# The sign of float64 weights carried through a rounding step, and newly written instruction lists, in a GateLoop and maxout kernel

## The chip, the cores and the metric

The kernel runs on one core of one Trainium2 chip. The metric is the device time of one execution in microseconds (us), lower is better. The profiled execution is a single one, recorded on that core.

## The reference, cut to what matters

First a GateLoop attention block: for each of 4 batches and 8 heads, over 768 positions with head size 48, a complex gate `a` (real part `a_re`, imaginary part `a_im`) is normalised, and a 48 x 48 state is turned and shrunk by it and added to.

```python
mag = np.sqrt(a_re * a_re + a_im * a_im)
scale = np.minimum(mag, 0.999) / (mag + 1e-06)
a_re_n, a_im_n = (a_re * scale, a_im * scale)
...
S_re, S_im = (new_re + kv, new_im)
y[:, :, t] = np.einsum('bhd,bhde->bhe', q[:, :, t], S_re)
```

Then its output, laid out as 3072 tokens of 384 features, goes through a feed-forward block that takes the larger of three products (384 to 768) and multiplies it by a fourth matrix (768 to 384).

```python
h = np.maximum(np.maximum(x @ w1, x @ w2), x @ w3)
return (h @ w_out).astype(np.float32)
```

The four weight matrices arrive as float64 (a float32 draw times a float64 scalar), so the kernel has to turn them into float32 by itself. [...]

## The kernel before, in words

**Tiling.** A group `g` (0 to 11) is 64 positions of all heads; a group has two halves `c` (x and y), of two batches each. For a group the kernel computes the gates (logarithms, exponentials, an arctangent) on 128 x 768 tiles, then turns q and k by running sums of the angles, forms masked scores in blocks (A, B), the outputs y, the state update dk, and then the feed-forward block: up projections `U`, maxima `u`, and the down projection by seven half-size products (Strassen's scheme: sums `S`, products `P`, result additions `r`). Group 0 goes through plain projections instead (`U..x`, `U..y`, `Ox`, `Oy`), with its two halves apart, since it starts while weights are still being prepared. The maximum is rewritten: w2 and w3 are replaced by their differences to w1, and w1 is multiplied into the output matrix in advance (entries `T`, `t`, `M`, `m`).

**Order of the work.** Nothing is scheduled by the hardware or by a loop. The string `SCHEDULE` (L21) lists about 1,750 entries of the form `name:group`. `run` (L972) takes them in order, and each emits one or more instructions. `Bound` (L187 to L205) ties each instruction to the one before it on the same engine, so the list is the order of every engine's queue: PE, DVE, ACT, POOL, and SP for most loads. An engine waits at the head of its own queue until the operands are there. All instructions pass through one helper line, so the profile puts them all at L198, and they are told apart by tile names. `SLOTS` (L116) names the PSUM slot of each successive product. `OTHER` (L122) is the set of entries that use their second choice of engine: copies out of PSUM, absolute values and the maximum with zero go to DVE in place of ACT; loads of q, k and v are issued by POOL in place of SP; additions of one tile to another are done by DVE in place of an accumulating DMA issued by POOL.

**Weights.** The weights come in twelve blocks of 128 x 768 values (`WL0` to `WL11`), each loaded as pairs of 32-bit words (768 KB) into a room that is free at the time (`ROOMS`, L129; the room called S is the tile `strassen`, H is `xhx`). `weight_step` (L419) then makes float32 of each pair with bit operations, in five steps. A high word, read as a float32, has the sign, 8 of the 11 exponent bits, and the upper mantissa.

- `Wa` (ACT): absolute value of the high word, times 2^-112, which takes the exponent offset off; it reads every second word of the room and writes a dense scratch tile `ex`.
- `Wb` (DVE): minimum with a constant, dense, in place.
- `Wc` (DVE): shift left by 3 (for blocks 0, 3 and 6, which are wanted negative, the sign bit is set as well).
- `We` (DVE): the low word shifted right by 29 is or-ed in; it reads every second word.
- `Wf` (DVE): the sign bit of the high word is xor-ed in, and the result is written to its place.
- `Wg` (six of the blocks): the block of w1 is added, by POOL's DMA or by DVE.

**Other entries that the prediction speaks of.** `Lnop` and `addw` are additions in the gates that go by accumulating DMA or DVE; `Q1`, `Q2`, `QB`, `KB`, `QG` scale copies of Q and K on DVE; `Kc` and `Qc` copy the transposed K and Q out of PSUM; `Ox:0` is the second plain output projection of group 0; the final entries `ox`, `oy`, `oz` add the last products into the output tile and `Dx`, `Dy`, `Dz` store it.

Of the kernel before, what the change touches and what calls it, by code (L numbers as in the profile page):

```python
# [21 lines left out]
Lix:0 sqi0:0 Zf:0 Zg:0 Lrx:0 xor0:0 sqr0:0 Liy:0 Lry:0 sqi1:0 add0:0 lnL0:0 expe0:0 expw0:0 xor1:0 lne0:0 relu0:0  # L22
Lnop0:0 WL0:0 sqr1:0 Wa0:0 add1:0 CL:0 lnL1:0 expe1:0 Lkx:0 abs0:0 Lix:1 Wb0:0 Wc0:0 We0:0 WL3:0 half0:0 expw1:0 Fx:0
lne1:0 relu1:0 Lnop1:0 pw0:0 Wa3:0 Wf0:0 abs1:0 Wb3:0 half1:0 WL6:0 lnw0:0 expL0:0 f3x:0 Liy:1 f2x:0 Lrx:1 Wc3:0 Wa6:0
f1x:0 Lry:1 mulai0:0 mulw0:0 We3:0 Wb6:0 WL9:0 pw1:0 lnw1:0 stt0:0 expL1:0 mulw1:0 f0x:0 atan0:0 mulai1:0 Wf3:0 T0:0
sqi:1 stt1:0 turn0:0 Wc6:0 atan1:0 Lqy:0 sumsx:0 csx:0 turn1:0 We6:0 Lqx:0 sqr:1 add:1 Wf6:0 Wa9:0 Wb9:0 WL11:0 WL10:0
xor:1 Enx:0 Eqx:0 lnL:1 Wc9:0 Ekx:0 tx:0 relu:1 mkx:0 csy:0 expe:1 We9:0 nfx:0 expw:1 sumsy:0 Lix:2 ty:0 Wf9:0 abs:1
T2:0 nfy:0 mqx:0 half:1 afx:0 Wa10:0 Wa11:0 Lvy:0 t2:0 Wb10:0 Wb11:0 Wc10:0 Wc11:0 We10:0 sax:0 We11:0 pw:1 sbx:0
uqx:0 tpqx:0 lnw:1 t0:0 Wf11:0 WL1:0 T1:0 WL2:0 Wf10:0 expL:1 Qcx:0 Lky:0 ukx:0 tpkx:0 mulw:1 Wa1:0 t1:0 Cdx:0 Lvx:0
Eqy:0 Kcx:0 Wa2:0 lne:1 Q2x:0 Fy:0 f2y:0 Wb1:0 f1y:0 WL4:0 kEnx:0 Q1x:0 M0:0 f3y:0 Liy:2 f0y:0 Eny:0 mulai:1 Wb2:0  # L30
afy:0 Ax:0 Wc1:0 stt:1 We1:0 mqy:0 Wc2:0 Wf1:0 We2:0 Eky:0 say:0 QBx:0 sqi:2 KBx:0 Lnop:1 sby:0 Wa4:0 Wf2:0 g0x:0
dkx:0 Lrx:2 Lry:2 sqr:2 add:2 atan:1 lnL:2 Wb4:0 Cdy:0 turn:1 WL5:0 Wg1:0 Wc4:0 M1:0 h1x:0 expe:2 cs:1 relu:2 g1x:0
Liy:3 expw:2 t:1 Wa5:0 abs:2 lne:2 We4:0 g2x:0 mky:0 Wf4:0 uky:0 M2:0 g3x:0 Bx:0 Wb5:0 nfx:1 Wc5:0 m1:0 Z3:0 b1x:0
tpky:0 Zh:0 uqy:0 nfy:1 b0x:0 tpqy:0 We5:0 Wg4:0 Lix:3 F:1 Kcy:0 yx:0 Lqy:1 Qcy:0 Wf5:0 xor:2 m0:0 Q2y:0 xx:0 addw:2
Q1y:0 KBy:0 WL7:0 f1:1 f0:1 QBy:0 Wg2:0 sumsx:1 Enx:1 WL8:0 half:2 Cdx:1 Ekx:1 Cdy:1 U11x:0 u11x:0 Lqx:1 lnw:2 Ay:0
Wa7:0 g0y:0 Eqx:1 expL:2 af:1 U01x:0 Wb7:0 f2:1 u01x:0 U02x:0 g1y:0 By:0 mulai:2 Wg5:0 g2y:0 Wc7:0 Wa8:0 g3y:0 We7:0
b0y:0 Lky:1 b1y:0 kEny:0 Wf7:0 sumsy:1 f3:1 yy:0 mulw:2 xy:0 sb:1 dky:0 u02x:0 stt:2 U02y:0 Lkx:1 h1y:0 Z4:0 mqx:1
atan:2 U11y:0 Lnop:2 Wb8:0 mkx:1 turn:2 sa:1 ukx:1 u11y:0 U01y:0 U12y:0 u01y:0 Eky:1 uqx:1 u02y:0 Eqy:1 cs:2 u12y:0
tpqx:1 Wc8:0 We8:0 mky:1 Eny:1 Lky:2 tpkx:1 Qcx:1 Wf8:0 t:2 Wg7:0 U21y:0 Wg8:0 U21x:0 nfy:2 nfx:2 Q1x:1 Lqx:2 mqy:1
Q2x:1 kEnx:1 uqy:1 u21y:0 U22y:0 u22y:0 u21x:0 af:2 Kcx:1 sumsx:2 F:2 Ax:1 g0x:1 g1x:1 g2x:1 Ekx:2 Enx:2 Eqx:2 Z2:0  # L40
Lvx:1 f1:2 f3:2 KBx:1 h0x:1 uky:1 tpqy:1 f2:2 Qcy:1 Q1y:1 g3x:1 Oy:0 Lvy:2 tpky:1 Q2y:1 mqx:2 Lvy:1 f0:2 Lkx:2 sa:2
sqi:3 oy:0 Lry:3 J3:0 QBx:1 dkx:1 Bx:1 sb:2 h1x:1 U12x:0 QBy:1 uqx:2 QGx:1 U22x:0 Kcy:1 KBy:1 Lrx:3 Lqy:2 u22x:0
u12x:0 Ay:1 b1x:1 g0y:1 g1y:1 g2y:1 g3y:1 b0x:1 mkx:2 sqr:3 tpqx:2 Qcx:2 By:1 yx:1 add:3 lnL:3 QBx:2 expe:3 b0y:1
sumsy:2 xx:1 Eqy:2 Eky:2 expw:3 relu:3 Q1x:2 b1y:1 QGy:1 abs:3 Ox:0 Q2x:2 Lix:4 ukx:2 ox:0 mky:2 mqy:2 Dy:0 uky:2 yy:1
addw:3 tpky:2 lne:3 kEny:1 tpkx:2 Liy:4 Lnop:3 xy:1 xor:3 half:3 Cdy:2 Kcy:2 U11:1 Cdx:2 J1:0 U01:1 Lqx:3 Lrx:4 uqy:2
lnw:3 Kcx:2 KBx:2 J2:0 expL:3 u11:1 Dx:0 Eny:2 mulw:3 mulai:3 stt:3 kEny:2 h0y:1 tpqy:2 atan:3 Lry:4 sqi:4 turn:3
Qcy:2 dky:1 h1y:1 kEnx:2 sumsx:3 u01:1 J4:0 cs:3 Eqx:3 mqx:3 Ax:2 h0y:2 Ekx:3 t:3 sqr:4 add:4 g0x:2 g1x:2 g2x:2 U12:1
Enx:3 Lrx:5 nfx:3 U02:1 lnL:4 expe:4 Q1y:2 nfy:3 expw:4 u12:1 S3:1 af:3 dky:2 g3x:2 relu:4 abs:4 addw:4 Q2y:2 F:3
u02:1 Bx:2 Ay:2 Lvx:2 sb:3 S1:1 f2:3 Lkx:3 h1y:2 f1:3 QGx:2 Lqy:3 P5:1 S2:1 P7:1 f0:3 QBy:2 g0y:2 KBy:2 g1y:2 f3:3
S4:1 lnw:4 g2y:2 P1:1 expL:4 h0x:2 P6:1 r1:1 b0x:2 b1x:2 g3y:2 r6:1 dkx:2 r5:1 r7:1 lne:4 Lry:5 sa:3 Lky:3 r57:1 h1x:2  # L50
sumsy:3 By:2 xor:4 mkx:3 b1y:2 b0y:2 Eny:3 half:4 Cdy:3 Liy:5 yx:2 xx:2 mulw:4 Eky:3 Eqy:3 Py:1 QGy:2 Px:1 P4:1 P3:1
yy:2 ukx:3 uqx:3 xy:2 oy:1 tpkx:3 tpqx:3 mky:3 h0x:3 mulai:4 Kcx:3 Lix:5 sqi:5 stt:4 Qcx:3 Lqx:4 Lky:4 P2:1 uky:3
Lnop:4 atan:4 U01:2 ox:1 u01:2 tpky:3 Lvy:3 QGx:3 Kcy:3 mqy:3 Cdx:3 uqy:3 tpqy:3 turn:4 sumsx:4 Qcy:3 Lrx:6 kEny:3
KBx:3 h0y:3 Lkx:4 Q2y:3 QBx:3 Ekx:4 Enx:4 Q1y:3 Eqx:4 cs:4 F:4 f1:4 mkx:4 t:4 sqr:5 U11:2 u11:2 Lqx:6 f3:4 Q2x:3 f2:4
Dy:1 nfx:4 Q1x:3 nfy:4 Ay:3 add:5 g0y:3 Ax:3 f0:4 g0x:3 g1y:3 g2y:3 af:4 mqx:4 xor:5 Bx:3 g3y:3 sb:4 KBy:3 U02:2 sa:4
g1x:3 U12:2 ukx:4 u02:2 S3:2 g2x:3 tpkx:4 g3x:3 Lvx:3 uqx:4 Lvy:4 lnL:5 expw:5 relu:5 Lqy:4 u12:2 expe:5 Kcx:4 tpqx:4
Qcx:4 dky:3 kEnx:3 dkx:3 S1:2 h1y:3 sumsy:4 S2:2 P5:2 h1x:3 Eqy:4 QBy:3 Dx:1 abs:5 Liy:6 addw:5 b0x:3 b1x:3 lne:5
Lnop:5 half:5 Eky:4 mky:4 Eny:4 mqy:4 Cdx:4 S4:2 Cdy:4 P1:2 P6:2 Py:2 P4:2 r1:2 yx:3 r6:2 r5:2 By:3 lnw:5 expL:5 b0y:3
mulw:5 uqy:4 h0x:4 b1y:3 mulai:5 QGy:3 Px:2 stt:5 atan:5 Lix:6 P3:2 Lry:6 xx:3 sqr:6 Liy:7 P7:2 r7:2 Lkx:5 uky:4 P2:2
tpqy:4 Lky:5 Qcy:4 r57:2 tpky:4 yy:3 sqi:6 ox:2 Lqx:5 kEnx:4 kEny:4 Lvx:4 dkx:4 oy:2 add:6 xy:3 Kcy:4 sumsy:5 turn:5  # L60
sumsx:5 h1x:4 QGx:4 Dy:2 Dx:2 Ekx:5 cs:5 Q1y:4 lnL:6 Lix:7 Eqx:5 U11:3 mkx:5 expw:6 Lvx:5 relu:6 KBx:4 Q2x:4 Enx:5
expe:6 lne:6 h0y:4 Q2y:4 mqx:5 Eky:5 U01:3 Lnop:6 abs:6 Q1x:4 u11:3 t:5 nfy:5 nfx:5 Eny:5 QBx:4 u01:3 Eqy:5 mky:5
xor:6 Ax:4 af:5 g0x:4 addw:6 sb:5 dky:4 h1y:4 sa:5 F:5 half:6 f3:5 uqx:5 g1x:4 g2x:4 lnw:6 expL:6 U12:3 u12:3 f2:5
Lrx:7 f0:5 f1:5 U02:3 tpqx:5 g3x:4 mulai:6 uky:5 tpky:5 Qcx:5 mulw:6 u02:3 Lqy:5 S1:3 Ay:4 Bx:4 S2:3 P1:3 QBy:4 sqi:7
S3:3 mqy:5 b1x:4 P5:3 Kcy:5 b0x:4 KBy:4 g0y:4 P6:3 stt:6 g1y:4 uqy:5 By:4 atan:6 yx:4 ukx:5 P7:3 g2y:4 g3y:4 Lkx:6
Lry:7 sqr:7 QGy:4 b0y:4 b1y:4 Cdy:5 Cdx:5 Q1x:5 tpkx:5 xx:4 Kcx:5 turn:6 tpqy:5 add:7 S4:3 Qcy:5 Lvx:6 r1:3 yy:4 xy:4
sumsx:6 Eqx:6 cs:6 t:6 lnL:7 r6:3 Px:3 kEnx:5 r5:3 Q2x:5 Py:3 P4:3 Enx:6 h0x:5 Ekx:6 xor:7 nfy:6 kEny:5 P2:3 U01:4
r7:3 nfx:6 expw:7 dkx:5 expe:7 lne:7 relu:7 abs:7 r57:3 addw:7 QGx:5 af:6 Lry:8 Lvy:5 h1x:5 mqx:6 sb:6 Lqy:6 u01:4
sumsy:6 QBx:5 sa:6 F:6 Liy:8 U11:4 f3:6 Eqy:6 mkx:6 Q2y:5 Eky:6 KBx:5 mqy:6 P3:3 Lky:6 Q1y:5 f1:6 uqy:6 Lrx:8 h0y:5
f0:6 oy:3 Eny:6 ox:3 Bx:5 u11:4 KBy:5 lnw:7 Ax:5 g0x:5 Ay:5 g1x:5 half:7 g2x:5 expL:7 f2:6 g3x:5 mulai:7 U02:4 g0y:5  # L70
g1y:5 g2y:5 b0x:5 g3y:5 QBy:5 b1x:5 mky:6 yx:5 ukx:6 By:5 Lvy:6 Dx:3 Cdy:6 u02:4 Cdx:6 QGy:5 mulw:7 b1y:5 uqx:6 U12:4
P1:4 S3:4 b0y:5 P7:4 stt:7 atan:7 Lqx:7 xx:5 u12:4 S1:4 tpqx:6 tpkx:6 S2:4 Kcx:6 yy:5 turn:7 Lnop:7 dky:5 Qcx:6 uky:6
Lkx:7 r1:4 sqr:8 sumsx:7 xy:5 h1y:5 cs:7 t:7 kEnx:6 Lix:8 sqi:8 P6:4 Px:4 Py:4 P5:4 P2:4 P4:4 QBx:6 Dy:3 h0x:6 add:8
lnL:8 relu:8 Q1x:6 expw:8 nfx:7 Q2x:6 Eqx:7 expe:8 S4:4 nfy:7 P3:4 tpqy:6 r6:4 KBx:6 Lqx:8 abs:8 Liy:9 r5:4 r7:4 Ekx:7
r57:4 tpky:6 ox:4 oy:4 Enx:7 af:7 dkx:6 Qcy:6 kEny:6 F:7 Dx:4 sa:7 xor:8 h1x:6 half:8 sb:7 h0y:6 Lkx:8 Dy:4 f0:7 f2:7
Q2y:6 f1:7 QGx:6 U11:5 u11:5 Cdx:7 mkx:7 U12:5 Kcy:6 u12:5 Q1y:6 Lry:9 Cdy:7 U01:5 Lrx:9 Lix:9 mqx:7 addw:8 f3:7 ukx:7
# [994 lines left out]
```

## Time and profile before

| | us |
|---|---|
| three timed runs | 549.97, 552.18, 553.06 (median 552.18) |
| profiled execution, its span | 550.3 |
| median less that span | 1.9 |
| PE busy | 515.6 |
| DVE busy | 484.8 |
| ACT busy | 363.8 |
| POOL busy | 115.6 |

The page gives no other time for the profiled execution than its span, from the first to the last instruction. The span is 1.9 us under the median of the runs and lies between the fastest and the slowest. Busy time is the union of an engine's instructions; the row of a group gives the number of instructions, their summed time, the mean of one in ns, and the idle time of the engine in front of them with what released it. In a table of stretches the columns are the stretch, its length, the busy time of PE, of PE's weight loads, of DVE, ACT and POOL (with instruction counts), the granted PE clock as a share of full speed, the DMA share, and GB/s.

### The profile page before, as it was taken

What the parts mean: (1) busy time and instruction counts of PE and PEld (TensorE: products, weight loads), DVE (VectorE), ACT (ScalarE), POOL (GpSimd) and SP (SyncE); (2) the same over time, 40 slices, a digit from 0 to 9 for tenths busy, and PEclk for the clock granted to TensorE, in tenths of its full rate; (3) what the DMA queues carried; (4) which work ended last, traced back from release to release, by engine and by line L of the source; (5) the groups of instructions that cost most, each with busy time, mean ns of one, the idle gap of its engine ahead of it and who ended that gap; (6) DMA issues with size and microseconds to landing.
All of it is one profiled execution on the core that took longest, in us unless ns stands there. A gap on an engine that the chain in (4) does not pass through costs nothing.

```text
span 550.3 us, 22368 instructions
## 1 busy us (share of the span) xinstructions
PE 515.6 (94%) x9998; PEld 441.4 (80%) x9998; DVE 484.8 (88%) x735; ACT 363.8 (66%) x568; POOL 115.6 (21%) x167
## 2 busy tenths in 40 slices
...
GB/s 233 243 206 170 244 129 89 101 92 69 80 89 74 96 111 104 49 91 83 104 42 121 3 52 107 64 105 112 22 104 11 66 117 2 4 30 4 2 29 29
DMA packets 117023, 47.93 MB, mean 87 GB/s; under 512 B 103936, under 2 KB 109536, under 8 KB 116928
## 3 DMA queue, kind: packets, MB, share of 16 engines
...
q0 software_dynamic: 10304, 14.05, 14.1%
q8 instruction: 78, 1.28, 0.9%
...
q14 instruction: 17, 0.14, 0.1%
...
## 4 chain that ended last, share of the span: by engine, by line
PE 71%; DVE 10%; issue 2%; ACT 1%; DVEq 0%; ACTq 0%
PE up L198 28%; PE op L198 22%; PE y L198 6%; PE tp L198 4%; PE A L198 3%; PE dk L198 3%; PE sums L198 2%; DVE atm L198 1%; PE B L198 1%; DVE Q L198 1%; PE F L198 1%; DVE QG L198 1%; PE cs L198 1%; DVE uk L198 1%; DVE xhx L198 1%
## 5 line engine op out<-in xcount | busy, mean ns | idle before, releaser
L198 PE MATMUL up<-xhx,w 128*128 128x256 f32 x792 | 177.5, 382 | 0.0
L198 PEld LDWEIGHTS up<-xhx,w 128*128 128x128 f32 x792 | 148.6, 190 | 22.4 <-DVE g L198 2.2
L198 ACT ACT_TABLE_LOAD x50 | 64.2, 1283 | 4.4 <-issue 3.6
L198 POOL DMA_DIRECT2D ar<-nf x44 | 39.9, 1297 | 77.8 <-DVE ar L198 66.7
L198 ACT COPY atm<-B 32x128 f32<-32x128 f32 x96 | 24.5, 256 | 39.4 <-DVE atm L198 24.2
L198 PE MATMUL op<-wo,xhx 128*128 128x192 f32 (+1 forms) x220 | 49.2, 362 | 0.0
L198 DVE TENSOR_TENSOR Q<-Q,f 112x1024 f32<-112x1024 f32 (+1 forms) x48 | 45.3, 951 | 0.4 <-ACT Q L198 0.2
L198 PE MATMUL y<-atm,vb 128*32 128x64 f32 x1152 | 39.4, 221 | 2.9 <-issue 2.9
L198 PEld LDWEIGHTS op<-wo,xhx 128*128 128x128 f32 x220 | 36.7, 190 | 3.3 <-issue 0.6
L198 PEld LDWEIGHTS y<-atm,vb 128*32 128x32 f32 x1152 | 33.1, 110 | 7.3 <-issue 6.2
L198 PE MATMUL y<-QG,g 112*32 112x64 f32 x1408 | 37.3, 220 | 0.5 <-issue 0.5
L198 DVE TENSOR_TENSOR ot<-ot,op 128x192 f32<-128x192 f32 (+1 forms) x67 | 27.1, 413 | 11.0 <-PE op L198 6.2
L198 DVE TENSOR_TENSOR xhx<-xhx,up 128x768 f32<-128x768 f32 x22 | 20.9, 951 | 17.9 <-PE up L198 17.9
L198 PEld LDWEIGHTS y<-QG,g 112*32 112x32 f32 x1408 | 34.6, 110 | 0.7 <-issue 0.7
L198 PE MATMUL op<-wo,strassen 128*128 128x192 f32 x176 | 34.2, 339 | 0.1
L198 POOL DMA_DIRECT2D w<-L x8 | 9.0, 1124 | 117.4 <-ACT L L198 104.8
L198 PE MATMUL op<-w,strassen 128*128 128x192 f32 x176 | 32.8, 329 | 0.0
L198 DVE COPY_PREDICATED atm<-masko,A 128x256 f32<-128x256 uint8 x72 | 31.2, 435 | 1.2
L198 PEld LDWEIGHTS op<-wo,strassen 128*128 128x128 f32 x176 | 30.0, 196 | 2.3 <-issue 0.7
L198 PE MATMUL A<-Q,K 112*32 112x80 f32 x1536 | 30.6, 234 | 0.5 <-issue 0.5
L198 PEld LDWEIGHTS op<-w,strassen 128*128 128x128 f32 x176 | 28.9, 190 | 1.9 <-ACT ot L198 0.8
L198 PEld LDWEIGHTS A<-Q,K 112*32 112x32 f32 x1536 | 27.4, 110 | 3.6 <-issue 1.4
...
## 6 DMA issues: line engine op xcount, KB each, us to landing
...
w<-in_moe_w_dram SPq DMA_DIRECT2D x3, 768.0 KB, 7.0
```

The lines of the kernel that those rows point to most:

```text
L198: ins = f(*a, **kw)
```

## The change

The weight conversion drops one of its five steps. `Wb` now comes first and limits the signed high word to plus and minus a constant; it reads the room itself, every second word, and writes `ex`. `Wa` comes second, dense and in place: a parametric ReLU with the scale 2^-112 (negative for the blocks that are wanted negative) and a slope of -2^32 for negative values, so that a negative input comes out positive with one more exponent bit set, which the shift of `Wc` moves into the sign's place. `Wc` is then one shift for all blocks, and `We` writes the result to its place. `Wf` is gone. The constant is the largest high word that fits float32 in place of its scaled image.

The three lists are written anew: `SCHEDULE` has 1,740 entries in place of 1,752, the twelve `Wf` being the only names that are gone and none being added; `SLOTS` still has 258 digits, in another order; in `OTHER` 34 entries are gone and 48 are new. Among the new ones are `abs1:0`, `abs:1`, `afy:0`, `af:1`, `Qcx:0`, `u11x:0` and `addw:10`; `Wg4:0` is gone. Loads of q, k and v that POOL issues go from 27 entries to 37.

```diff
-    LAST = float(np.array(0x0FEFFFFF, dtype=np.int32).view(np.float32))
+    LAST = float(np.array(0x47EFFFFF, dtype=np.int32).view(np.float32))
...
-        if step == "a":
-            activation(out=ex.bitcast(FP), in_=high.bitcast(FP), func=AF.Abs, scale=2.0 ** -112)
-        elif step == "b":
-            dve.tensor_single_scalar(out=ex.bitcast(FP), in_=ex.bitcast(FP), scalar=LAST, op=OP.min)
+        if step == "b":
+            dve.tensor_scalar(out=ex.bitcast(FP), in0=high.bitcast(FP), scalar1=LAST, scalar2=-LAST, op0=OP.min, op1=OP.max)
+        elif step == "a":
+            activation(out=ex.bitcast(FP), in_=ex.bitcast(FP), func=AF.Prelu, alpha=-2.0 ** 32,
+                       scale=-2.0 ** -112 if i in (0, 3, 6) else 2.0 ** -112)
         elif step == "c":
-            if i in (0, 3, 6):
-                dve.tensor_scalar(out=ex, in0=ex, scalar1=3, scalar2=-0x80000000, op0=OP.logical_shift_left,
-                                  op1=OP.bitwise_or)
-            else:
-                dve.tensor_single_scalar(out=ex, in_=ex, scalar=3, op=OP.logical_shift_left)
+            dve.tensor_single_scalar(out=ex, in_=ex, scalar=3, op=OP.logical_shift_left)
         elif step == "e":
-            dve.scalar_tensor_tensor(out=ex, in0=low, scalar=29, in1=ex, op0=OP.logical_shift_right, op1=OP.bitwise_or)
-        elif step == "f":
-            dve.scalar_tensor_tensor(out=dst.bitcast(I32), in0=high, scalar=-0x80000000, in1=ex,
-                                     op0=OP.bitwise_and, op1=OP.bitwise_xor)
+            dve.scalar_tensor_tensor(out=dst.bitcast(I32), in0=low, scalar=29, in1=ex, op0=OP.logical_shift_right,
+                                     op1=OP.bitwise_or)
```

Four places of the lists, cut out (the rest of the lists is of the same kind). Around block 10:

```diff
-ty:0 Wf9:0 abs:1 T2:0 nfy:0 mqx:0 half:1 afx:0 Wa10:0 Wa11:0 Lvy:0 t2:0 Wb10:0 Wb11:0 Wc10:0 Wc11:0 We10:0
+nfx:0 relu:1 We9:0 WL2:0 csy:0 expe:1 expw:1 Wb10:0 ty:0 Wb11:0 abs:1 Lrx:2 Wa10:0 nfy:0 half:1 afx:0 Wa11:0
```

Around the second plain output projection:

```diff
-sumsy:2 xx:1 Eqy:2 Eky:2 expw:3 relu:3 Q1x:2 b1y:1 QGy:1 abs:3 Ox:0 Q2x:2 Lix:4 ukx:2 ox:0 mky:2 mqy:2 Dy:0
+sumsy:2 g2y:1 Lky:2 Lqy:2 g3y:1 sqr:3 Eqy:2 b0y:1 add:3 kEny:1 xx:1 Ox:0 Eky:2 QGy:1 mqy:2 lnL:3 mky:2 uqy:2
```

Around the gate addition of group 10, which `OTHER` now gives to DVE:

```diff
-expe:10 lne:10 abs:10 nfy:9 addw:10 u01:7 U02:7 Ekx:9 half:10 u02:7 Bx:8 Ax:8 Ay:8
+expe:10 abs:10 lne:10 Lry:11 Lix:11 Ekx:9 nfy:9 af:9 u01:7 addw:10 mkx:9 Ax:8 lnw:10
```

At the end:

```diff
-P6:11 kEny:11 P3:11 r6:11 r5:11 ox:11 P7:11 P4:11 r7:11 r57:11 Dx:11 oy:11 Dy:11 oz:11 Dz:11
+P6:11 Px:11 P3:11 P2:11 P4:11 r6:11 r5:11 r7:11 r57:11 oz:11 ox:11 oy:11 Dz:11 Dx:11 Dy:11
```

More of the change, by code (lines that the diff above doesn't have):

```diff
@@ L21 @@
 SCHEDULE = """
[L22 to L76, printed above, removed]
@@ new lines @@
+mulai0:0 Lry:1 mulw0:0 lnw1:0 WL9:0 Wb3:0 stt0:0 half1:0 f3x:0 expL1:0 WL11:0 Wa3:0 WL10:0 mulw1:0 Wa6:0 atan0:0
+mulai1:0 Wc3:0 Lqx:0 stt1:0 mqx:0 sqi:1 sqr:1 We3:0 atan1:0 Wc6:0 We6:0 Lkx:0 Lqy:1 add:1 lnL:1 turn0:0 Wb9:0 csx:0
+Wa9:0 turn1:0 mkx:0 xor:1 WL1:0 tx:0 Wc9:0 nfx:0 relu:1 We9:0 WL2:0 csy:0 expe:1 expw:1 Wb10:0 ty:0 Wb11:0 abs:1 Lrx:2
+Wa10:0 nfy:0 half:1 afx:0 Wa11:0 Wc10:0 CL:0 sbx:0 sax:0 Wc11:0 afy:0 We10:0 uqx:0 ukx:0 pw:1 lne:1 Wb1:0 Lky:0 tpqx:0
+Qcx:0 Cdx:0 Lry:2 Lqy:0 tpkx:0 We11:0 lnw:1 Lnop:1 f1x:0 kEnx:0 T0:0 WL4:0 Cdy:0 T2:0 expL:1 Kcx:0 Liy:2 mulw:1 t2:0
@@ new lines @@
+QGx:1 Q2y:1 Ekx:2 Lvx:2 af:2 g0x:1 uky:1 Oy:0 Q1y:1 f2:2 KBx:1 f0:2 QBx:1 g1x:1 f1:2 h0x:1 Eqx:2 f3:2 Lvx:1 sb:2 tpky:1
+sa:2 Liy:3 g2x:1 Lqx:2 dkx:1 mqx:2 oy:0 Kcy:1 g3x:1 Bx:1 sqi:3 mkx:2 h1x:1 Ay:1 U12x:0 U22x:0 b1x:1 uqx:2 b0x:1 KBy:1
+QBy:1 u12x:0 tpqx:2 J3:0 u22x:0 By:1 Lrx:3 Lry:3 Dy:0 g0y:1 g1y:1 Z3:0 Qcx:2 yx:1 Lix:4 sumsy:2 g2y:1 Lky:2 Lqy:2 g3y:1
+sqr:3 Eqy:2 b0y:1 add:3 kEny:1 xx:1 Ox:0 Eky:2 QGy:1 mqy:2 lnL:3 mky:2 uqy:2 b1y:1 Lvy:1 Lrx:4 expw:3 expe:3 relu:3
+lne:3 Q2x:2 Lnop:3 Eny:2 yy:1 ox:0 uky:2 abs:3 J1:0 tpky:2 ukx:2 xor:3 addw:3 half:3 Q1x:2 J2:0 xy:1 Lkx:3 lnw:3 expL:3
@@ new lines @@
+b1y:4 Cdy:5 Liy:8 QGy:4 Q1x:5 tpkx:5 tpqy:5 P7:3 Lqx:6 Cdx:5 Q2x:5 turn:6 Kcx:5 Lix:8 Lqy:6 Lky:6 Qcy:5 lnL:7 xor:7
+Lkx:6 kEny:5 kEnx:5 Lry:8 Py:3 Q1y:5 P4:3 S4:3 yy:4 cs:6 Px:3 relu:7 t:6 xx:4 expw:7 nfx:6 P2:3 xy:4 P3:3 U01:4 Lvy:5
+r6:3 r5:3 expe:7 nfy:6 r7:3 abs:7 r57:3 af:6 lne:7 QGx:5 dkx:5 Q2y:5 sb:6 h0x:5 QBx:5 sa:6 u01:4 ox:3 oy:3 sumsy:6
+Eqy:6 h1x:5 sumsx:6 Eny:6 Ekx:6 F:6 f3:6 mqy:6 Eqx:6 mkx:6 half:7 Dx:3 addw:7 U11:4 f1:6 Eky:6 f0:6 Ay:5 lnw:7 ukx:6
+expL:7 mqx:6 KBx:5 mky:6 f2:6 Enx:6 uqx:6 Ax:5 u11:4 mulw:7 Lnop:7 g0y:5 Lvy:6 g0x:5 g1x:5 g2x:5 Cdy:6 Bx:5 KBy:5 uqy:6
```

126 lines of the change are left out of this document (82 added, 44 removed).

## The prediction

> **What bounds the kernel now.** I read first the busy time of each engine by stretch, cut at the first matmul (10.77 us), at the second plain output projection (110.03 us) and at 495 us.
>
> ```profile
> 0.00:10.77 10.77, 0.00 (x0) 0.03 (x1) 6.83 (x24) 5.80 (x11) 8.21 (x36) 1.00 0.84 192
> 10.77:110.03 99.26, 82.43 (x1480) 59.61 (x1480) 96.39 (x150) 89.15 (x142) 33.16 (x41) 0.90 0.80 175
> 110.03:495.00 384.97, 382.00 (x7879) 335.79 (x7876) 357.63 (x522) 264.88 (x405) 74.20 (x91) 1.00 0.37 72
> 495.00:550.30 55.30, 51.17 (x645) 45.96 (x643) 23.94 (x41) 3.98 (x12) 0.00 (x0) 1.00 0.07 16
> ```
>
> The reader sees two kernels. From 110 us on PE is busy 382.0 of 385.0 us, then 51.2 of 55.3, so there the time is PE's work plus 3.0 us of gaps plus a tail of 4.1. Before 110 us PE is idle for 10.8 + 16.8 = 27.6 us, and its clock is 0.90; there DVE is busy 96.4 of 99.3 us and ACT 89.2. So a microsecond taken from DVE or ACT moves the end only if it lies before 110 us, and only as far as the other of the two lets it.
>
> The waits of PE, read next, name who held it, and the group rows show that the only long gap behind 110 us is of another kind.
>
> ```profile
> PE cs L198 <- DVE w L198: 3.7, 1, 3.7
> PE sums L198 <- ACT E L198: 3.0, 1, 3.0
> PE cs L198 <- ACT g L198: 2.9, 1, 2.9
> PE tp L198 <- DVE uq L198: 1.4, 1, 1.4
> PE y L198 <- issue: 3.4, 3, 2.6
> ```
>
> DVE and ACT share the blame about evenly; DMA, at a share of 0.80, is the third resource that is nearly used up before 110 us.
>
> **The change part by part.** *The five steps become four.* The rows of the old steps:
>
> ```profile
> L198 DVE TENSOR_SCALAR xhx<-xhx 128x768 f32<-128x768 f32 x12 | 6.7, 558 | 0.4 <-ACT xhx L198 0.4
> L198 DVE TENSOR_SCALAR xhx<-xhx 128x768 int32<-128x768 int32 x12 | 6.8, 574 | 0.0
> L198 DVE SCALAR_TENSOR_TENSOR xhx<-w,xhx 128x768 int32<-128x768 int32 x4 | 3.8, 949 | 0.0
> L198 DVE SCALAR_TENSOR_TENSOR ai<-ar,ai 128x768 int32<-128x768 int32 x11 | 10.5, 951 | 0.0
> L198 ACT ACTIVATE xhx<-w 128x768 f32<-128x768 f32 x4 | 3.6, 905 | 0.0
> L198 ACT ACTIVATE L<-ar 128x768 f32<-128x768 f32 x8 | 6.7, 843 | 0.1
> L198 ACT ACTIVATE Ln<-L,biases 128x768 f32<-128x768 f32 x11 | 10.2, 932 | 0.0
> 37.21 0.95 DVE L198 SCALAR_TENSOR_TENSOR wo<-w,xhx 128x768 int32<-128x768 int32 x1
> 38.08 0.94 DVE L198 SCALAR_TENSOR_TENSOR wo<-strassen,xhx 128x768 int32<-128x768 int32 x1
> 38.95 0.95 DVE L198 TENSOR_TENSOR uk<-CS,k 128x768 f32<-128x768 f32 x1
> ```
>
> `Wf` is one of the 0.95 us rows; on a busy DVE such instructions start 0.87 us apart (37.21, 38.08, 38.95), so twelve of them take 12 x 0.87 = **10.4 us of DVE**. `Wc` loses nothing: its row has blocks with one operation and with two, at one mean of 574. `Wb` now reads every second word and does two operations. No row shows that form on DVE with one input; it lies between 0.56 (the dense row) and 0.95 (the strided steps, which are no slower than the dense `ai<-ar,ai`: 949 against 951). Since the stride costs nothing in the second pair I take 0.56, and keep 12 x 0.39 = 4.7 us for the range. [...] `Wa` turns from the strided 0.905 to the dense 0.843, 0.06 x 12 = 0.7 us less on ACT, if the parametric ReLU costs what other functions do; the dearest ACT row of that size, with an operand per partition, is 0.932, which bounds it at 1.1 us more.
>
> *What stands ahead of the point where PE takes over.* I compare the two lists at `Ox:0`.
>
> ```profile
> 110.03 2.20 PE L198 MATMUL op<-wo,xT 128*128 128x384 f32 x6
> L198 DVE COPY Q<-tp 112x1024 f32<-112x1024 f32 x6 | 7.3, 1219 | 0.4 <-PE tp L198 0.4
> L198 DVE TENSOR_SCALAR L<-ar 128x768 int32<-128x768 int32 x3 | 1.7, 556 | 1.0 <-ACT Ln L198 1.0
> L198 ACT COPY Q<-tp 112x1024 f32<-112x1024 f32 x18 | 18.3, 1017 | 3.4 <-PE tp L198 3.2
> L198 ACT ACTIVATE e<-L 128x768 f32<-128x768 f32 x11 | 9.3, 844 | 0.1
> L198 DVE TENSOR_TENSOR QG<-Q,f 112x1024 f32<-112x1024 f32 x22 | 26.8, 1219 | 3.9 <-PE y L198 3.9
> L198 DVE TENSOR_TENSOR QB<-Q,f 112x512 f32<-112x512 f32 x24 | 16.4, 685 | 0.2 <-PE B L198 0.2
> ```
>
> PE has exactly the same entries ahead of `Ox:0` in both. On DVE twelve `Wf` and `Wg4` go (11.3), and `QBx:2`, `Q1x:2`, `QGy:1` now stand behind it (0.6 + 0.6 + 1.1); in come `Qcx:0` (1.1), `abs:1` and `af:1` (0.5 each), three half-size ones of that kind (`abs1:0`, `afy:0`, `u11x:0`, 0.3 each) and `kEny:1` (0.9), prices start to start, about 0.08 under the rows. That is 13.6 - 3.9 = **9.8 us less** (with the unrounded prices). On ACT the six entries that went to DVE give 3.5, the twelve `Wa` 0.7, and seven entries of groups 1 to 3 (five of the 0.84 to 0.93 kind) now stand behind, 4.8: **8.9 us less**. Behind `Ox:0` DVE has as much left as before, so nothing is merely put off at PE's cost there.
>
> *The wait that is added.* `Wa` used to wait for the block's landing, on ACT; now `Wb` does, on DVE, and everything on DVE is queued behind it. It matters for block 10.
>
> ```profile
> 10.00:20.00 10.00, 6.84 (x62) 4.21 (x62) 9.93 (x19) 9.68 (x19) 9.63 (x17) 1.00 1.02 272
> 17.02 0.47 SPq L198 DMA_DIRECT2D strassen<-in_moe_w_out_dram  x1
> strassen<-in_moe_w_out_dram SPq DMA_DIRECT2D x1, 768.0 KB, 14.1
> 31.18 0.92 ACT L198 ACTIVATE xhx<-strassen 128x768 f32<-128x768 f32 x1 [0.28 <-DMA strassen<-in_moe_w_out_dram]
> 32.14 0.56 DVE L198 TENSOR_SCALAR xhx<-xhx 128x768 f32<-128x768 f32 x1 [0.16 <-ACT xhx L198]
> ```
>
> It landed at 17.02 + 14.1 = 31.1 us. The new list puts the same loads ahead of it on SP, and one 192 KB pair less on POOL, some 0.7 us at the 272 GB/s to be had there, so an estimate is 30.4. DVE came to `Wb10` at 32.1; in the new list it has four `Wf` and about a microsecond of other work less ahead of it, 4.3 us, so it arrives at 27.8 and waits 30.4 - 27.8 = **2.6 us**. ACT's `Wa10` follows it: it would come 1.8 us earlier than its 31.2 - 0.3, at 29.1, and can start at 30.4 + 0.6 = 31.0, so ACT loses 1.9 of its 8.9. What stays is 9.8 - 2.6 = 7.2 by DVE and 7.0 by ACT. With the two level, each catches the other's waits; I take off a microsecond and count **6.0 us**.
>
> *The long gap behind 110 us.* At 427.8 us PE stops inside the 224 short instructions of a `y`, waiting for nothing that the profile shows, while DMA is full:
>
> ```profile
> 424.38 0.94 POOL L198 DMA_DIRECT2D w<-L  x1 [30.91 <-ACT L L198]
> 426.36 1.34 POOL L198 DMA_DIRECT2D Ln<-e  x1
> 430.41 0.25 PE L198 MATMUL y<-atm,vb 128*32 128x64 f32 x2 [2.60 <-issue]
> 428.00:429.00 1.00, 0.00 (x0) 0.00 (x0) 0.40 (x1) 0.99 (x2) 0.00 (x0) 1.00 0.96 107
> 431.00:432.00 1.00, 1.00 (x65) 1.00 (x56) 0.00 (x0) 0.00 (x0) 0.00 (x0) 0.70 0.43 84
> 433.00:434.00 1.00, 1.00 (x4) 1.00 (x4) 1.00 (x2) 0.96 (x3) 0.00 (x0) 0.50 0.00 0
> ```
>
> I read it as instructions that came late behind the data. PE then runs four microseconds at 0.70, 0.50, 0.50 and 0.60, so it costs 2.6 + 1.7 = 4.3 us. [...] The new list gives `addw:10`, that first `w<-L`, to DVE, so one 384 KB transfer leaves this crowd; but loads are re-dealt everywhere and another `y` may be hit. Ends: 4.3 gone, or nothing. No row decides; I take half, **2.2 us**.
>
> *The tail.* After the last product (544.70 + 1.46) two additions follow, then the store. The new end puts `oz` ahead of the last product's addition, so one of the two is hidden: **0.3 us**.
>
> ```profile
> 544.70 1.46 PE L198 MATMUL op<-w,xhx 128*128 128x192 f32 x8
> 546.21 0.62 DVE L198 TENSOR_TENSOR ot<-ot,op 128x192 f32<-128x192 f32 x2 [0.56 <-PE op L198]
> ```
>
> *At nothing:* the table loads. By the lists they fall from 50 to 36, but both have eleven ahead of `Ox:0`; the fourteen lie where ACT is busy 265 of 385 us, and PE covers them. If that cover failed, they would be 14 x 1.28 = 18 us of ACT. The ten more loads by POOL are about 1 us each on an engine busy 74 of 385 us.
>
> **Sum.** 6.0 + 2.2 + 0.3 = 8.5 us; the span goes from 550.3 to 541.8, and the median, 1.9 above that span, from 552.2 to **543.7 us**.
>
> **The rivals.** *ACT or the DMA takes over* (chance 0.20): DVE's gain is real but PE's start is then set by ACT's chain or by landings, which are level with DVE already; summed at the same prices, the lists promise only 2.5 us at the worst point I found (the first up projection of group 1 has 108.3 us of DVE entries ahead of it in the new list and 110.8 in the old, with PE work equal within half a microsecond). With the gap at 427 us back elsewhere, 552.2 - 2.5 - 0.3 = 549.4.
>
> *DVE waits for the weights* (0.13, slower): `Wb` at the head of the busiest queue. Each of blocks 9, 11, 10, 1 and 2 is asked for about 3 to 4 us earlier; if each keeps DVE for 2.6, it is 13 us, against 9.8 saved and 0.3 of tail: 552.2 + 2.9 = 555. It decides from 10 us of such waits on. Against it: one DMA backlog is waited out only once.
>
> *New gaps in the long stretch* (0.14): the list does not do what it was re-dealt for; a few more stops of the 4.3 us kind, or late loads, eat the 6 us: 552 on both sides.
>
> *The new function needs a table of its own* (0.03): a pair of loads around each run of `Wa`, up to 12 x 2 x 1.28 = 31 us of ACT before 110 us; 552 + 31 - 8 = 575.
>
> ```profile
> L198 ACT ACT_TABLE_LOAD x50 | 64.2, 1283 | 4.4 <-issue 3.6
> ```
>
> [...]
>
> **How the numbers follow.** The forecast as worked out has 0.50, from 537.5 (both engines' 7.2, the whole 4.3, and some of the other idle time) to 547. Faster by over 0.5% (about what a measurement of this kernel can tell from no change), under 549.4: 0.50, half of the first rival, a quarter of the third: 0.64. Within: 0.10 + half of the third, 0.07: 0.17. Slower, over 554.9: 0.13 + 0.03 + the rest of the third, 0.03: 0.19. The range runs from 537.5 to 553.5; it leaves out the slower rivals and a little below.
>
> **What would show it.** Right: DVE busy falls by about 10 us; the row `f32 x12` of `Wb` stays near 558; 50 table loads become 36; the second plain projection starts near 104 us; DVE has one wait on a DMA near 28 to 30 us; no `issue` gap over a microsecond. Wrong: a `Wb` row near 950, ACT waiting nowhere before 104 us, or several DVE waits on weight DMAs.

## The result, and the profile after

The changed kernel takes 569.31 us (median of 568.82 to 570.76) against 551.69 for the kernel before beside it: 1.0335 times as long, interval 1.0304 to 1.0367. The forecast, 543.7 us with 537.5 to 553.5, was wrong in sign. The profiled execution has a span of 567.5 us, 17.2 more than before.

The instruction groups of the changed kernel show that the parts did what was priced (count, then busy time and mean in ns, then idle time in front):

```profile
L196 ACT ACT_TABLE_LOAD x36 | 46.2, 1283 | 4.2 <-issue 3.6
L196 ACT ACTIVATE xhx<-xhx 128x768 f32<-128x768 f32 x12 | 9.8, 835 | 1.1 <-DVE xhx L196 1.1
L196 DVE TENSOR_SCALAR xhx<-w 128x768 f32<-128x768 f32 x4 | 2.2, 551 | 0.0
L196 DVE TENSOR_SCALAR xhx<-strassen 128x768 f32<-128x768 f32 x3 | 1.7, 557 | 1.1 <-DMA strassen<-in_moe_w_out_dram 1.1
```

`Wb`, two operations on every second word, is as quick as the dense one was (551 and 557 ns, before 558); `Wa` needs no table of its own, with 36 table loads in all; DVE waits 1.1 us for block 10. DVE's busy time fell from 484.8 to 475.3 us, ACT's from 363.8 to 341.1, and PE's stayed (515.6, 515.3). So all of the loss is idle time of PE: 34.7 us before, 52.2 after. The same view as the prediction's first, cut at the second plain projection, now at 109.64 us:

```profile
0.00:10.77 10.77, 1.14 (x2) 0.50 (x2) 7.34 (x25) 5.84 (x12) 8.65 (x32) 1.00 0.83 225
10.77:109.64 98.87, 77.85 (x1479) 57.23 (x1478) 88.44 (x142) 84.02 (x135) 37.50 (x52) 0.91 0.85 181
109.64:495.00 385.36, 369.81 (x7646) 323.55 (x7643) 340.52 (x503) 245.91 (x392) 83.52 (x105) 0.99 0.36 69
```

Up to the projection DVE is busy 95.8 us where it was 103.2 (the first two rows added), 7.4 less, and ACT 89.9 where it was 95.0; the projection starts only 0.4 us earlier, so the time saved became idle time of these engines. From 110 to 495 us PE is idle for 15.6 us, where it was 3.0. The waits of PE in the changed kernel have rows that the list before had not at all, products (`op`) that wait for result readings (the entries `r` and `o`, which copy or add a product out of PSUM into the output tile `ot`):

```profile
PE op L196 <- DVE ot L196: 9.3, 4, 5.8
PE op L196 <- ACT ot L196: 3.4, 5, 1.7
PE F L196 <- issue: 3.3, 1, 3.3
PE tp L196 <- ACT atm L196: 1.1, 1, 1.1
```

And the timeline has these places (start, duration; in brackets the idle time in front):

```profile
64.13 0.28 PE L196 MATMUL F<-cuts,Ln 64*48 64x29 f32 x4 [3.29 <-issue]
438.37 0.24 PE L196 MATMUL y<-atm,vb 128*32 128x64 f32 x1 [0.76 <-issue]
441.69 1.46 PE L196 MATMUL op<-w,strassen 128*128 128x192 f32 x8
444.93 1.46 PE L196 MATMUL op<-wo,strassen 128*128 128x192 f32 x8
445.24 0.84 ACT L196 ACTIVATE L<-w 128x768 f32<-128x768 f32 x1
446.49 0.35 DVE L196 TENSOR_TENSOR ot<-ot,op 128x192 f32<-128x192 f32 x1 [6.55 <-ACT L L196]
455.69 0.55 DVE L196 TENSOR_TENSOR ot<-ot,op 128x384 f32<-128x384 f32 x1
456.29 2.93 PE L196 MATMUL op<-wo,strassen 128*128 128x192 f32 x8 [5.80 <-DVE ot L196]
560.50 1.46 PE L196 MATMUL op<-w,xhx 128*128 128x192 f32 x8
562.01 1.08 DVE L196 TENSOR_TENSOR ot<-ot,op 128x192 f32<-128x192 f32 x3 [2.97 <-PE op L196]
```

The stop at 427 us, 2.60 us before, is down to 0.76 (438.37). But in group 8 PE stops 5.80 us at `P3:8`, and the clock falls behind that stop (the next to last three figures are clock, DMA share, GB/s):

```profile
456.00:457.00 1.00, 0.71 (x2) 0.71 (x3) 1.00 (x2) 0.00 (x0) 0.93 (x2) 0.50 0.00 0
...
460.00:461.00 1.00, 1.00 (x4) 0.82 (x3) 0.97 (x2) 0.00 (x0) 0.12 (x1) 0.50 0.76 192
461.00:462.00 1.00, 1.00 (x5) 0.83 (x5) 1.00 (x2) 0.00 (x0) 0.00 (x0) 0.92 0.77 205
```

The 0.7 us of work in the first of these microseconds and the four behind it go at half speed, which is another 2.4 us, so this one place costs 8.2.

### The profile page after: what moved, and what is told of

Its sections match the earlier page's. It is cut to its first block, busy times and chain, and to the rows that moved or that the text cites. A ratio compares the mean times of both kernels' runs of the same rounds, so it can differ in the third digit from the quotient of the medians.

```text
span 567.5 us, 22382 instructions
## 1 busy us (share of the span) xinstructions
PE 515.3 (91%) x9998; PEld 441.1 (78%) x9998; DVE 475.3 (84%) x727; ACT 341.1 (60%) x549; POOL 129.7 (23%) x188
## 4 chain that ended last, share of the span: by engine, by line
PE 46%; DVE 5%; issue 2%; ACT 1%; DVEq 0%; ACTq 0%
PE up L196 21%; PE op L196 13%; PE y L196 3%; PE A L196 3%; PE tp L196 2%; PE dk L196 1%; DVE ot L196 1%; PE sums L196 1%; PE B L196 1%; DVE uk L196 1%; PE F L196 1%; ACT f L196 1%; DVE strassen L196 1%; DVE g L196 0%; PE cs L196 0%
## 5 line engine op out<-in xcount | busy, mean ns | idle before, releaser
L196 POOL DMA_DIRECT2D ar<-nf x44 | 44.0, 1369 | 78.2 <-DVE ar L196 65.4
L196 ACT COPY Q<-tp 112x1024 f32<-112x1024 f32 x21 | 21.1, 1011 | 34.9 <-PE tp L196 34.8
L196 POOL DMA_DIRECT2D k<-in_k_dram x28 | 22.1, 886 | 63.8 <-DVE uk L196 63.4
L196 ACT ACTIVATE xhx<-up 128x768 f32<-128x768 f32 x15 | 12.1, 808 | 36.7 <-PE up L196 36.7
```

The costliest lines, as they stand in the source:

```text
L196: ins = f(*a, **kw)
```

## The experiments

All in one table: the median time, its ratio to the kernel before beside it (with the interval), the profiled span, the start of the second plain projection there, and what is left from there to the end, which separates front and rest. Spans, starts and rests are of one profiled execution each, which lies up to 3.2 us from its kernel's median: the changed kernel and the five below that share its list, slots and engines up to this projection (products first, group 8 mended, `r6:8` later, `oy:8` later, group 8 and products first) start it at 107.60 to 109.82 us. Differences of 2 or 3 us in these columns say little. The last kernel was timed twice only.

| kernel | median us | ratio | span | start | rest |
|---|---|---|---|---|---|
| before | 550.2 to 551.7 | | 550.3 | 110.03 | 440.3 |
| changed | 569.3 | 1.0335 (1.0304-1.0367) | 567.5 | 109.64 | 457.9 |
| conversion alone | 558.0 | 1.0126 (1.0083-1.0168) | 556.2 | 116.28 | 439.9 |
| conversion alone, places swapped | 557.2 | 1.0132 (1.0089-1.0175) | 553.0 | 114.61 | 438.4 |
| lists alone | 583.9 | 1.0592 (1.0548-1.0637) | 581.8 | 124.24 | 457.6 |
| new front, old rest | 556.5 | 1.0095 (1.0070-1.0120) | 555.2 | 110.09 | 445.1 |
| new front to 83 us, old rest | 557.0 | 1.0087 (1.0058-1.0117) | 553.2 | 109.77 | 443.4 |
| old front, new rest | 584.9 | 1.0607 (1.0554-1.0659) | 583.2 | 116.80 | 466.4 |
| changed, old `OTHER` | 584.5 | 1.0619 (1.0579-1.0659) | 583.1 | 110.48 | 472.6 |
| changed, products first | 566.0 | 1.0285 (1.0239-1.0330) | 562.8 | 107.60 | 455.2 |
| changed, group 8 mended | 562.4 | 1.0212 (1.0174-1.0250) | 560.7 | 109.39 | 451.3 |
| changed, `r6:8` later | 568.1 | 1.0306 (1.0251-1.0362) | 569.6 | 109.82 | 459.8 |
| changed, `oy:8` later | 565.4 | 1.0244 (1.0185-1.0304) | 562.7 | 107.69 | 455.0 |
| changed, group 8 and products first | 563.5 | 1.0212 (1.0189-1.0235) | 562.2 | 108.64 | 453.6 |
| before less `Wf` | 553.2 | 1.0032 (1.0014-1.0049) | 553.6 | 114.62 | 439.0 |
| before less `Wa` | 551.6 | 1.0008 (0.9985-1.0032) | 550.6 | 110.62 | 440.0 |
| before less both | 548.4 | 0.9939 (0.9909-0.9968) | 544.7 | 105.79 | 438.9 |
| changed, three additions less | 570.9 | 1.0345 (1.0284-1.0407) | 571.8 | 108.51 | 463.3 |

### Conversion or lists

```diff
-Wa6:0 ... Wb6:0 ... We6:0 ... Wf6:0     (old lists)
+Wb6:0 Wa6:0 ... We6:0                   (conversion alone; all twelve blocks)
+Wb6:0 ... Wa6:0 ... We6:0               (places swapped)
-Wb6:0 ... Wa6:0 ... We6:0               (new lists)
+Wa6:0 ... Wb6:0 ... We6:0 Wf6:0         (lists alone, with the old steps)
```

> The old lists with the new four-step conversion alone: the twelve Wf are taken out, and each Wb stands directly ahead of its Wa. Theory (the new order behind the second plain output projection makes the loss, the conversion is a gain): DVE busy falls by 9 to 11 us, the second plain projection starts 2 to 7 us earlier than at 110.0, time 544 to 550 us. Rival (the conversion itself makes the loss, since DVE now waits for landings or ACT for DVE): time 560 us or more, and DVE rows in front of 110 us that wait for a weight DMA or for ACT's scratch tile for over 10 us in sum.

> The old lists with the new conversion, but each Wb at the old place of Wa and each Wa at the old place of Wb, so that the distance between the two steps stays. Theory (the 7.7 us that ACT waited for Wb with the two side by side made that kernel slow): ACT waits under 3 us for DVE's scratch tile, the second plain projection starts 2 to 8 us ahead of 116.3, time 548 to 555 us. Rival (DVE itself is held at Wb, by landings or by its other queue, or ACT's Wa comes too late for Wc): time 556 us or more, DVE waiting on ACT's scratch tile.

> The new lists with the old five-step conversion: Wa and Wb change places, and each Wf stands directly behind its We. Theory (the loss is in the new lists): DVE has 10 us more ahead of the second plain projection than in the changed kernel, so time 570 to 580 us, with the PE gaps behind 110 us of the changed kernel (15.6 us) still there. Rival (the conversion makes the loss): about 552 us.

The theory holds for the rest: it lasts 438 to 440 us with the old order and 458 with the new, whichever the conversion (the lists alone took 4 us more than forecast). It fails for the front: the conversion by itself, in the old list, is no gain but a loss of 1.3%, by either placing. A block now goes from DVE to ACT and back to DVE, where it went once from ACT to DVE. With `Wb` directly ahead of `Wa`, ACT waits; with the places swapped, DVE waits. The waits up to 118 us, first of the one kernel, then of the other:

```profile
ACT xhx L197 <- DVE xhx L197: 7.7, 6, 2.1
```

```profile
DVE xhx L197 <- ACT xhx L197: 4.7, 6, 1.8
```

In the changed kernel little of this is left (1.2 us for DVE, 1.1 for ACT), and in its list the four steps are worth 14.6 us of the start (124.24 against 109.64). But that only reaches what the old list, with its own steps, had already: 110.03.

### The two halves of the list, and the second choices of engine

The hybrids take one list up to an entry and then what is left in the order of the other, with PSUM slots given out anew. The last kernel keeps the new lists with the old `OTHER`.

```diff
+Lix:0 Zf:0 Lrx:0 ... xx:1 Ox:0 | Lvy:1 lnL:3 QBx:2 ...     (new front, old rest)
+Lix:0 Zf:0 Lrx:0 ... Eky:1 Lnop:2 | Liy:3 Z3:0 mky:1 ...   (new front to 83 us, old rest)
+Lix:0 sqi0:0 Zf:0 ... abs:3 Ox:0 | Liy:4 Lqx:3 Lvx:2 ...   (old front, new rest)
```

> New conversion; the new list up to and with the second plain output projection, then what is left in the order of the old list, with PSUM slots given out anew behind that point. Theory (the order of the rest makes the loss): PE idle behind 110 us back to 3 to 6 us, time 548 to 554 us. Rival (the new front puts work off or spoils the landings, so that PE pays for it later whatever the order): PE idle behind 110 us stays at 12 us or more, time 560 to 568 us.

> New conversion; the new list up to and with Lnop:2, which is directly behind the last weight block, then what is left in the order of the old list (the two lists have almost the same entries up to there: seven differ). Theory (the new order is a loss only behind the weights): the second plain projection starts at 104 to 109 us, PE idle behind it is 4 to 8 us, time 544 to 551 us. Rival (every seam of the two orders costs as much as the first hybrid's): time 554 us or more.

> New conversion; the old list (with Wf taken out) up to and with the second plain output projection, then what is left in the order of the new list. Theory (the order of the rest makes the loss): PE idle behind that point stays at 10 us or more with waits of the output products on DVE's and ACT's result additions (ot), time 557 to 565 us. Rival (the new front makes the loss): 544 to 550 us.

> The changed kernel with the old set of second choices of engine (copies, absolute values, additions and issues of loads as before). Theory (the order of result readings makes the loss): the waits of the output products on ot stay at 9 us or more, time 564 to 575 us. Rival (the new division among the engines makes it: more loads by POOL, other copies by DVE): the waits go, time 552 to 560 us.

With the old order behind it the new front leads to a rest of 443 to 445 us, 13 to 15 less than in the changed kernel, so most of the loss sits in the new order behind 110 us. Both times are above the forecast of the theory, and the rest is 3 to 5 us longer than in the kernel before; whether that is the seam, where one order meets the other, or something that the new front leaves behind isn't shown. The new rest behind the old front has the same waits of products on readings (9.2 and 3.4 us) and more, for 584.9 us in place of the 557 to 565 expected; the old `OTHER` leaves them (9.8 and 3.4) and adds others, for 584.5 us. So the new division among the engines isn't the cause: with the old one the new order is slower still.

### The result readings

What the prediction did not see, and these traces show: a reading of a product tile starts only when every product of the tile ahead of it in the list is done, and a product waits for every reading ahead of it, whichever quarter either uses. `r6:8` adds the quarter of `P6:8`, done at 443.15 (441.69 + 1.46), and starts 0.10 us behind the end of `P5:8` (444.93 + 1.46), another quarter. The profile puts this wait down to ACT's `L`, but that was done at 446.08 (445.24 + 0.84), 0.41 us ahead, and is no operand of `r6:8`; in the kernels with group 8 mended, with `r6:8` later and with `oy:8` later, too, `r6:8` starts 0.10 us behind the end of `P5:8`. While DVE stood there 6.55 us, four entries that needed nothing from it queued behind `r6:8`; 10 us later PE met the late `oy:8`, a reading from the other product tile, which holds up `P3:8` there: it ends at 456.24 (455.69 + 0.55), and `P3:8` starts at 456.29.

```diff
 products first:   r1, r6, r5, oy behind the last product of their tile (groups 1-6, 8, 9, 11)
 group 8 mended:
-f0:10 r6:8 QGy:9 mkx:10 f2:10 ukx:10 mky:10 r5:8 ... uky:10 oy:8 stt:11 P3:8 U11:9
+f0:10 QGy:9 mkx:10 f2:10 ukx:10 mky:10 r6:8 r5:8 ... uky:10 stt:11 P3:8 oy:8 U11:9
```

> The changed kernel with eleven groups of result readings moved: where the new list puts a reading of one of the two product tiles (r1, r6, r5, oy) ahead of a later product of the same tile, the reading now stands directly behind that product. Nothing else moves. Theory (a product waits for every reading of its tile that stands ahead of it in the list, and in the new order these readings are late): the waits of the output products on DVE's and ACT's ot, 12.7 us in the changed kernel, fall under 3 us, and the time falls by 8 to 13 us to 556 to 561 us. Rival (DVE and ACT are late by themselves in the new order, so PE meets the next late operand instead): time 565 us or more, with new PE waits of over 8 us on DVE or ACT.

> The changed kernel with two readings of group 8 moved: r6:8 behind ukx:10 and mky:10, directly ahead of r5:8, so that these no longer stand behind DVE's 6.55 us wait; and oy:8 behind P3:8 in place of ahead of it. Theory: the stop of 5.80 us at 456 us falls under 1.5 us and the time falls by 4 to 6 us, to 563.5 to 565.5 us. Rival (the stop moves to the next product): time within 2 us of 569.3.

> The changed kernel with only r6:8 moved, directly ahead of r5:8; oy:8 stays ahead of P3:8. Theory (what counts is that QGy:9, mkx:10, ukx:10 and mky:10 no longer stand behind DVE's 6.55 us wait): the stop of 5.80 us falls under 2.5 us, time 564 to 566 us. Rival (what counts is that P3:8 need not wait for oy:8): no change, 568 us or more.

> The changed kernel with only oy:8 moved, directly behind P3:8; r6:8 keeps DVE waiting. Theory: P3:8 then waits for S4:8, which came at 453.2 us, so the stop falls by 2 to 3 us and the time to 566 to 567.5 us. Rival (oy:8 alone was the cause): the whole stop goes, 562 to 564 us.

> The changed kernel with both edits of the result readings: products ahead of the readings of their tile (but oy:5 at its place), and r6:8 directly ahead of r5:8. Theory (a stop at the head of DVE's queue costs only where DVE's lead is needed soon after, and the two edits take out the places where this was so): time 556 to 560 us, PE idle behind 110 us under 9 us. Rival (DVE and ACT are late everywhere in the new order): no better than 562.4 us.

Mending group 8 took the stop away whole: 562.4 us, 6.9 less (more than expected, since the slow clock goes too: `P3:8` takes 1.57 us in place of 2.93). The timeline of that kernel, DVE and PE:

```profile
447.43 0.74 DVE L197 TENSOR_TENSOR ot<-ot,op 128x192 f32<-128x192 f32 x2 [3.21 <-ACT L L197]
...
451.36 1.57 PE L197 MATMUL op<-wo,strassen 128*128 128x192 f32 x8
```

DVE waits half as long, with the four entries done, and `P3:8` waits for nothing. Of the two moves alone, `oy:8` gave 3.9 us: `P3:8` then waits only for `S4:8`, 2.73 us. `r6:8` gave 1.2, which is within the spread of the runs (the intervals of the two ratios overlap), and less than its theory said: the stop fell only to 4.54 us. `oy:8` came only a little sooner, since DVE then waited 1.60 us for ACT on the way, and in this profile the clock fell elsewhere as well (to 0.50, behind a stop at 286 us). The first fence is of `oy:8` alone, the second of `r6:8` alone:

```profile
452.17 1.57 PE L197 MATMUL op<-wo,strassen 128*128 128x192 f32 x8 [2.73 <-DVE strassen L197]
```

```profile
457.82 0.69 PE L197 MATMUL op<-wo,strassen 128*128 128x192 f32 x1 [4.54 <-DVE ot L197]
```

So by these stops (5.80, 4.54, 2.73, none) the two readings are links of one chain, and both have to move. Putting products first everywhere missed its forecast: the 12.7 us of products waiting on `ot` went, and the time fell by only 3.3. That is no more than `oy:8` gives alone, and the move of `oy:8` is one of these, so the other moves gave nothing that can be measured. PE met the next late operand:

```profile
PE cs L197 <- DVE ot L197: 2.9, 1, 2.9
PE op L197 <- DVE strassen L197: 2.8, 2, 2.1
...
PE op L197 <- ACT K L197: 1.3, 1, 1.3
```

Both edits together (563.45 us) are no better than group 8 alone: behind the projection PE is idle for 18.2 us there and for 15.6 with group 8 alone (21.6 in the changed kernel, 7.1 before). The rival was right for all places but group 8: elsewhere DVE and ACT are late in the new order, and a late reading is only the first thing that PE sees of it.

### What sets the front

> The kernel before, with its own lists and its old conversion, but the step Wf left out and We writing the result; the weights lose their signs, so this part of the computation is left out. DVE has the same 10.4 us less as by the change, and the path of a block still goes once from ACT to DVE, in place of from DVE to ACT and back. Theory (the 10 us of DVE are worth most of their length ahead of the second plain projection, and the second crossing between the two engines takes them back): that projection starts at 102 to 106 us, time 543 to 548 us. Rival (DVE's time is not the bound there, so the forecast's 6 us were never to be had): it starts at 108 us or later, time 549 us or more.

> The kernel before, its lists and its conversion with the twelve Wa left out: Wb reads the high word itself, and the shift of Wc is by 0, so that the values stay finite; the weights are wrong, this part of the computation is left out. ACT has 12 x 0.9 = 10.9 us less ahead of the second plain projection, DVE has as much as before. Theory (ACT, busy 9.7 to 10.0 of each 10 us from 10 to 60 us, sets the front, so DVE's saving found nothing): that projection starts at 104 to 107.5 us, time 544 to 549 us. Rival (DVE and ACT both stand on the path, so one alone gives nothing): it starts at 108.5 us or later, and only the kernel without both comes earlier. Second rival (landings set the front): both kernels stay within 1.5 us of 110.

> As the kernel without Wa, with the twelve Wf left out as well: ACT 10.9 us and DVE 10.4 us less. Theory (ACT alone sets the front): within 1.5 us of the kernel without Wa. Rival (both stand on the path): the second plain projection starts at 100 to 105 us, 4 us or more ahead of the kernel without Wa, time 540 to 546 us. Second rival (landings, or PE's stops, set it): 108 us or later.

```diff
-We6:0 Wf6:0      (before less Wf: We writes to the block's place)
+We6:0
-Wa6:0 Wb6:0      (before less Wa: Wb reads the high word, Wc shifts by 0)
+Wb6:0
```

The theories of the first two fell. `Wf` left out alone (DVE busy 9.3 us less in all): no gain, the start even 4.6 later. `Wa` left out alone (ACT busy 9.0 us less): no gain. Both (8.4 and 9.3 us less): 4.2 us earlier, and the time 0.6% lower. One stretch of the windows view, 10 to 40 us, in that order of kernels behind the kernel before (PE, weight loads, DVE, ACT, POOL):

```profile
10.00:40.00 30.00, 18.69 (x130) 10.95 (x130) 29.49 (x49) 29.31 (x46) 14.50 (x22) 0.75 0.93 247
```

```profile
10.00:40.00 30.00, 17.33 (x125) 9.81 (x126) 24.66 (x42) 28.51 (x46) 13.68 (x21) 0.77 1.05 263
```

```profile
10.00:40.00 30.00, 18.40 (x146) 10.91 (x146) 29.80 (x49) 25.95 (x43) 14.85 (x21) 0.77 0.95 247
```

```profile
10.00:40.00 30.00, 20.55 (x184) 12.48 (x185) 28.44 (x47) 27.75 (x46) 14.48 (x21) 0.83 1.09 279
```

DVE and ACT are both busy for over 29 of 30 us before. With one relieved alone, the other stays nearly full (28.51 for ACT, 29.80 for DVE), and only with both relieved does PE get on (20.55 us in place of 18.69). The first rival (both on the path) is right in kind, though the two together gave 4.2 us in place of the 5 to 10 of its forecast. The 4.6 us of the kernel less `Wf` come late: its first y of `yx:0` starts at 65.58 us (before at 65.39, less `Wa` at 65.09, less both at 60.50). They come from a PE stop of 3.00 us in place of 0.53 in the A of group 1, an `issue` stop of the kind at 64.13, with six microseconds at a clock of 0.50 behind it. What makes these stops is the question to the last kernel, the changed one without `Wg4`, `Wg2` and `addw:2`:

```diff
+        if T["word"] in ("Wg4:0", "Wg2:0", "addw:2"):
+            return
```

> The changed kernel without three of its accumulating transfers (Wg2, Wg4 and addw:2, 384 KB each, issued at 52.7, 54.9 and 59.8 us); these additions are left out of the computation. Theory (the stop of 3.29 us inside F at 61 us, and the four slow microseconds behind it, come from transfers at a share over 1): the stop is under 0.5 us, the clock stays at 1.0 from 64 to 69 us, and the second plain projection starts 3 to 6 us ahead of 109.6. Rival (the stop is only slack, DVE and ACT set the start): the stop goes, but the projection starts at 108.5 to 110.5 us.

```profile
64.02 0.28 PE L197 MATMUL F<-cuts,Ln 64*48 64x29 f32 x4 [1.92 <-issue]
62.00:63.00 1.00, 0.10 (x8) 0.00 (x0) 0.95 (x2) 0.98 (x2) 0.00 (x0) 1.00 0.38 64
63.00:64.00 1.00, 0.00 (x0) 0.00 (x0) 0.69 (x1) 1.00 (x2) 0.00 (x0) 1.00 0.07 9
64.00:65.00 1.00, 0.98 (x52) 0.88 (x52) 0.95 (x2) 0.01 (x1) 0.00 (x0) 1.00 0.00 0
65.00:66.00 1.00, 1.00 (x25) 0.67 (x18) 1.00 (x2) 0.80 (x2) 0.00 (x0) 1.00 0.08 16
```

The DMA share in the stop is 0.38 and then 0.07 here (over 1.2 in the changed kernel), and PE still stops 1.92 us, at the same instruction. So full DMA is not needed for the stop, though it may lengthen it (3.29 with it). The stop is 1.4 us shorter and no slow clock follows, yet the start comes only 1.1 us earlier, which is within the spread given above: the stop was mostly slack, time that PE would have waited anyway. The rest of this kernel was 5 us longer, and the mean granted clock of the whole was 0.973 where the changed kernel had 0.978; one place of it is another stop of this kind (1.91 us at 187 us), with 0.50 from 189 to 192 us behind it.

## Why the prediction was wrong, step by step

- **What the operations cost: right.** `Wb` at 0.56, `Wa` without its own table, 36 loads, DVE and ACT down by what the lists said.
- **The failed step ahead of the projection: "What stays is 9.8 - 2.6 = 7.2 by DVE and 7.0 by ACT", counted as 6.0.** It paid out 0.4 in this profile, 0.2 to 2.4 in the six with this front. The time was saved (7.4 us of DVE, 5.1 of ACT), but did not move PE. The kernels that leave work out show the rate: over 9 us of DVE's busy time alone are worth nothing here, 8 to 9 us on both engines 4.2, so about half a microsecond for each and not the 6.0 of 7 that the prediction took. Its allowance for each engine catching the other's waits was one microsecond, where both were full from 10 to 40 us. And of the order of the two steps it priced only the wait for a landing (2.6, measured 1.1), not the second crossing between the engines, which made the conversion a loss in the old list.
- **The stop at 427 us: the reason wrong, the gain larger than counted.** It was to cost 4.3 us less or nothing, and half was taken, 2.2. At the same place (8,106 matmuls done before, 8,102 after) PE now stops 0.76 us and the clock stays at 1.00: 3.5 us less. But not because DMA was less full: its share is 1.00 from 437.6 to 438.4 us, where it was 0.97 in the stop before. Why the stop is shorter stays open, so this term was luck.
- **The tail: wrong sign.** Counted as 0.3 less. The last product starts 5.6 us ahead of the end before and 7.0 after: in the new end three readings stand behind it (the row at 562.01), since they wait for it as the last product of their tile. 1.4 us lost.
- **The step that was left out, and cost the most: the order of the readings and products behind 110 us.** The prediction compared how much work each engine has behind `Ox:0` and said that "nothing is merely put off at PE's cost there". What counts is who stands in front of whom. Its third rival ("the list does not do what it was re-dealt for") came nearest, with 0.14, but through more stops like that at 427 us or late loads, at 6 us; the rest behind the projection became 17.6 us longer.

Of these 17.6 us, 6.6 are shown to be group 8 (457.9 to 451.3 by the profiles), and 1.4 are read from the tail. For the other nearly 10 it is shown only that they go with the new order and not with the conversion: the old order behind the new front brings back 13 to 15. Which entries make them stays open; the other waits on readings that were taken out (products first) came back as waits at other places.

No kernel tried beats the one before except the one that leaves out both `Wf` and `Wa`.
